# Three pairs of buffers for the attention's result, three for the transposed probabilities, and an order computed anew

## The chip, the cores and the metric

The kernel runs on one core of a Trainium2 chip. The metric is the device time of one execution in microseconds (us); the median of the runs of a kernel is its time, lower is better. The core has TensorE (PE) for matrix products and transposes, VectorE (DVE), ScalarE (ACT) and GpSimd (POOL) for everything elementwise, and SyncE (SP), whose queue issues all transfers here. Each engine takes its instructions strictly in the order in which they were written.

## What is computed

A windowed attention feeds two feed-forward blocks. `x` of 2304 tokens by 512 passes from one to the next.

```python
def _attn_ref(q, k, v):                 # 4 x 8 heads x 576 x 64, a window of 64 positions
    scores = scale * np.matmul(q, k.transpose(0, 1, 3, 2))
    scores = np.where(mask, scores, -1000000000.0)
    attn = np.exp(scores - np.max(scores, axis=-1, keepdims=True))
    attn = attn / (np.sum(attn, axis=-1, keepdims=True) + 1e-09)
    return np.matmul(attn, v).astype(np.float32)

def _moe_ref(x, w_in, w_out, g_ln):     # 512 -> 1024 -> 512
    h = x @ w_in
    solu = h * softmax(h)
    ln = (solu - mu) / np.sqrt(var + 1e-06) * g_ln
    return (ln @ w_out).astype(np.float32)

def _moe2_ref(x, w_in, w_out, a, b):    # 512 -> 2048 -> 512
    P = a[0] + a[1] * h + a[2] * h2 + a[3] * h3
    Q = 1.0 + np.abs(b[0]) * np.abs(h) + np.abs(b[1]) * h2
    return ((P / (Q + 1e-06)) @ w_out).astype(np.float32)
```

The weights arrive as 64-bit floats and are turned into 32-bit ones on the chip.

## The kernel before

The tokens are cut into 18 tiles t of 128. One tile runs through these steps, whose names are the tiles that they write, with the tile's number behind them: the loads `q`, `k` (one each) and `v` (two, v0_0 and v0_1 for tile 0); the scores `s` on PE (L412 adds the mask, L418 the products); the maximum `mx` on DVE (L424), scaled on POOL (L428); eight exponentials `P` on ACT (L433); the sum on POOL (L438), its reciprocal `rc` on DVE (L442), and two halves of a normalization on POOL (L446); two transposes `pt` on PE (L452), copied to `PT` by ACT or DVE (L316, L318); the product with the values `pv` on PE (L472), whose first half needs v0_0 and whose second half needs v0_1; its copy to `xh` and, from tile 2 on, the rest `xl` = pv - xh on DVE (L312). `h` (L577 for tiles 0 and 1, L583 to L585 after) is the first feed-forward product, `st` and `e` (L591 to L633) its activation and layer norm, `pl` (L643) its transposes, `lh` and `ll` their copies. Every third tile closes with four products `x2` (L661 to L663), stored to DRAM. Then the second feed-forward block runs over six blocks of 384 tokens, with the products `hp` (L869 to L871) and `o` (L933 to L935) and an elementwise chain between them.

Beside this, ACT and DVE convert the weights: `xi` to `wi` (L524 to L551), `xo` to `co` and `wo` (L554, L562), and `xc` to `cc`, which go back to DRAM. Each such unit is two passes on ACT and four on DVE, of 1024 columns, and one or two more of each for the split in a high and a low part.

No engine's order is written by hand. `Schedule` (L25) gets every step with its engine, an assumed duration, what it needs, and the rings of buffers that it takes and gives; it works out due times, shifts them by a table of numbers (`SHIFT`, L169), and lets the steps run in a model of the engines. Steps are then written in the order of their modelled start. `RINGS` (L271) holds how many buffers each kind has: "x" is the pair `xh`, `xl` (taken by the step that writes pv, given back by the tile's last `h` product), "PT" the copied probabilities (two per tile, given back by pv), "k" and "q" have two each, given back by the scores, and "s", the scores, has one. A step that takes a buffer that is still held waits on the chip too, and so does everything behind it on its engine. The buffers for `xh` and `xl` stand in a pool of their own (`ax`, L328).

## Time and profile before

| what | before |
|---|---|
| median of 3 runs | 716.35 us (716.21 to 716.68) |
| the profiled execution | 717.4 us |
| its span, first to last instruction | 715.3 us |
| PE busy | 691.1 us (97%) |
| DVE busy | 575.5 us (80%) |
| ACT busy | 488.1 us (68%) |
| POOL busy | 89.0 us (12%) |

The busy times are shares of the span. PE is nearly always busy, so the questions are where the remaining microseconds of PE stand, and which engine ended each of those waits. A busy share over the whole span says little on that, since the stages differ: the first 80 us load, convert weights and run attention, the last 400 us are two products and their elementwise chain.

### The profile page before, as it was taken

The page shows a single profiled execution, that of the slowest core. Times are in us where ns is not written, and L with a number is a line of the kernel's source. Part 1 is how long each engine was busy: PE and PEld are TensorE (multiplying, and loading weights), DVE is VectorE, ACT ScalarE, POOL GpSimd, SP SyncE. Part 2 cuts the span into 40 slices and gives each one's busy share as a digit, 9 for nine tenths or more (in the row PEclk, how much of TensorE's full clock was granted, in tenths as well). Part 3 has the DMA queues.
Part 4 walks back from the last instruction along what each step waited for, and adds up shares of the span by engine and source line. Part 5 has one row for each costly group of instructions (what it writes and reads, how often), then busy time and mean ns, then how long its engine had stood idle before and what let it go on. Part 6 is the DMA issues. An engine that isn't in the chain of part 4 may idle for free.

```text
span 715.3 us, 11585 instructions
## 1 busy us (share of the span) xinstructions
PE 691.1 (97%) x4520; PEld 612.9 (86%) x4520; DVE 575.5 (80%) x713; ACT 488.1 (68%) x918; POOL 89.0 (12%) x142
## 2 busy tenths in 40 slices
PE   2889999999999999999999999999999999999998
PEld 1557899888898899998889988998898889989986
DVE  6899977898999735759998988798598869866973
ACT  6999967768868554748786665766486558555662
POOL 2553332243223220000000000000000000000000
PEclk9999999999999999999999999999999999999999
DMA  9864559668764314426301000200020000001001
GB/s 327 283 218 162 178 202 306 217 215 308 270 231 168 116 45 145 150 68 197 100 22 59 20 1 22 67 1 11 12 68 1 22 30 16 0 1 46 1 0 44
DMA packets 42741, 77.81 MB, mean 109 GB/s; under 512 B 4480, under 2 KB 22912, under 8 KB 42304
## 3 DMA queue, kind: packets, MB, share of 16 engines
q1 hardware_dynamic: 42688, 77.09, 32.1%
q8 instruction: 35, 0.57, 0.3%
q14 instruction: 18, 0.15, 0.1%
HBM read 59.25 MB, written 17.83 MB: 108 GB/s over the span
## 4 chain that ended last, share of the span: by engine, by line
PE 87%; DVE 5%; ACT 4%; DMA 2%; issue 1%; POOL 1%; DVEq 0%; ACTq 0%; POOLq 0%
PE hp L871 8%; PE hp L869 8%; PE hp L870 8%; PE o L935 8%; PE o L934 8%; PE o L933 8%; PE x L661 5%; PE x L663 5%; PE x L662 5%; PE h L583 4%; PE h L584 4%; PE h L585 4%; PE pv L472 3%; PE pl L643 2%; PE pt L452 2%; PE s L418 2%
## 5 line engine op out<-in xcount | busy, mean ns | idle before, releaser
L869 PE MATMUL hp<-x2h,w 128*128 128x384 f32 x384 | 129.4, 337 | 0.7 <-DVE t L902 0.5
L871 PE MATMUL hp<-x2h,w 128*128 128x384 f32 x384 | 129.3, 337 | 0.0
L870 PE MATMUL hp<-x2l,w 128*128 128x384 f32 x384 | 129.2, 337 | 0.0
L935 PE MATMUL o<-w,gl 128*128 128x512 f32 x282 | 111.5, 395 | 0.1
L934 PE MATMUL o<-w,gh 128*128 128x512 f32 x282 | 111.0, 394 | 0.0
L933 PE MATMUL o<-w,gh 128*128 128x512 f32 x282 | 110.7, 393 | 0.0
L879 ACT ACTIVATE w<-hp,ab 128x768 f32<-128x768 f32 x48 | 43.2, 900 | 70.5 <-PE hp L871 70.5
L887 DVE SCALAR_TENSOR_TENSOR w<-r,b,w 128x768 f32<-128x768 f32 x48 | 48.8, 1017 | 37.0 <-ACT r L881 36.9
L869 PEld LDWEIGHTS hp<-x2h,w 128*128 128x128 f32 x384 | 72.1, 188 | 4.0 <-PE hp L871 0.8
L870 PEld LDWEIGHTS hp<-x2l,w 128*128 128x128 f32 x384 | 72.1, 188 | 2.7
L871 PEld LDWEIGHTS hp<-x2h,w 128*128 128x128 f32 x384 | 72.1, 188 | 0.0
L917 ACT CAST gh<-t 128x768 fp32r<-128x768 f32 x48 | 40.1, 835 | 46.8 <-PE o L934 23.8
L661 PE MATMUL x<-lh,wo 128*128 128x384 f32 x192 | 66.7, 348 | 0.0
L663 PE MATMUL x<-lh,wo 128*128 128x384 f32 x192 | 65.0, 339 | 0.0
L662 PE MATMUL x<-ll,wo 128*128 128x384 f32 x192 | 65.0, 338 | 0.0
L935 PEld LDWEIGHTS o<-w,gl 128*128 128x128 f32 x282 | 52.9, 188 | 12.7 <-DVE gl L312 0.5
L934 PEld LDWEIGHTS o<-w,gh 128*128 128x128 f32 x282 | 52.9, 188 | 10.0
L933 PEld LDWEIGHTS o<-w,gh 128*128 128x128 f32 x282 | 53.0, 188 | 9.6
L312 DVE TENSOR_TENSOR gl<-t,gh 128x768 fp32r<-128x768 f32 x48 | 45.8, 954 | 13.8 <-ACT gh L917 13.8
L433 ACT ACTIVATE P<-s,mx 128x128 f32<-128x128 f32 x144 | 52.0, 382 | 2.4 <-POOL mx L428 2.4
L892 ACT ACTIVATE r<-w,qe 128x768 f32<-128x768 f32 x48 | 45.5, 947 | 9.7 <-DVE w L887 9.6
L583 PE MATMUL h<-wi,xh 128*128 128x512 f32 x128 | 50.8, 397 | 0.1
(112 smaller groups left out, 1465.5 us busy)
## 6 DMA issues: line engine op xcount, KB each, us to landing
v<-in_v_dram SPq DMA_DIRECT2D x35, 256.0 KB, 4.1
xc<-in_moe_w_in_dram SPq DMA_DIRECT2D x16, 512.0 KB, 4.4
xc<-in_moe_w_out_dram SPq DMA_DIRECT2D x16, 512.0 KB, 5.4
w2d<-cc SPq DMA_DIRECT2D x16, 512.0 KB, 3.5
r<-w2d SPq DMA_DIRECT2D x16, 512.0 KB, 4.0
k<-in_k_dram SPq DMA_DIRECT2D x17, 384.0 KB, 5.5
q<-in_q_dram SPq DMA_DIRECT2D x18, 256.0 KB, 5.6
x2d<-xs SPq DMA_DIRECT2D x6, 768.0 KB, 4.4
```

Source lines behind the costliest of these rows:

```text
L433: nc.scalar.activation(Pn[t][:, j, n, :], tiles["s", t][:, j, n, :], AF.Exp, bias=mx[:, c:c + 1], scale=0.125, accum_out=su[:, c:c + 1])
L583: nc.tensor.matmul(o, xh[:, c, :], wh, start=(c == 0), stop=False)
L661: nc.tensor.matmul(o, wh, lh[:, f, :], start=(f == 0), stop=False)
L662: nc.tensor.matmul(o, wh, ll[:, f, :], start=False, stop=False)
L663: nc.tensor.matmul(o, wl, lh[:, f, :], start=False, stop=(f == FC1 - 1))
L869: nc.tensor.matmul(h, wh[:, sl], xh[:, c], start=(c == 0), stop=False)
L870: nc.tensor.matmul(h, wh[:, sl], xl[:, c], start=False, stop=False)
L871: nc.tensor.matmul(h, wl[:, sl], xh[:, c], start=False, stop=(c == KC - 1))
L887: nc.vector.scalar_tensor_tensor(out=w, in0=r, scalar=b1, in1=w, op0=ALU.mult, op1=ALU.add)
L933: nc.tensor.matmul(o, gh[:, n, sl], wh, start=(f == 0), stop=False)
L934: nc.tensor.matmul(o, gh[:, n, sl], wl, start=False, stop=False)
L935: nc.tensor.matmul(o, gl[:, n, sl], wh, start=False, stop=(f == FC2 - 1))
```

## The change

The ring "x" grows from two to three pairs and its pool moves to another side of the on-chip memory, where it is closed together with the first feed-forward block. The ring "PT" shrinks from four to three. Some of the durations that the planner assumes are changed, and the table of shifts is another one, so that the order of every engine is another. What is computed, and how many instructions of each kind compute it, stays, apart from some copies that move between ACT and DVE.

```diff
 SHIFT = {
-    "zeros.0": 1.38, "load_q.0": 6.55, "load_k.0": -28.63, "load_v0.0": 141.12, "load_v1.0": -6.38,
...
+    "zeros.0": -13.05, "load_q.0": -5.7, "load_k.0": -7.11, "load_v0.0": 180.85, "load_v1.0": 15.6, "scores.0": 6.51,
...
-RINGS = {"q": 2, "k": 2, "v": 4, "s": 1, "P": 2, "tr": 2, "PT": 4, "o": 2, "x": 2, "h": 1, "e": 2, "lnT": 2, "xs": 1,
+RINGS = {"q": 2, "k": 2, "v": 4, "s": 1, "P": 2, "tr": 2, "PT": 3, "o": 2, "x": 3, "h": 1, "e": 2, "lnT": 2, "xs": 1,
...
-    ax = ctx.enter_context(tc.tile_pool(name="ax", bufs=2))
     ap = att.enter_context(tc.tile_pool(name="ap", bufs=2))
     mp = moe1.enter_context(tc.tile_pool(name="mp", bufs=2, side="right"))
+    ax = moe1.enter_context(tc.tile_pool(name="ax", bufs=3, side="right"))
...
-        PTs[t, j] = ap.tile([P, NPAIR, P], F32, name=f"PT{t}_{j}", tag="PT", bufs=4)
+        PTs[t, j] = ap.tile([P, NPAIR, P], F32, name=f"PT{t}_{j}", tag="PT", bufs=3)
...
-        step("max_scale", "POOL|DVE", (0.33, 0.18), ["max"], max_scale, t)
+        step("max_scale", "POOL|DVE", (0.5, 0.18), ["max"], max_scale, t)
...
-            step(f"norm{j}", "POOL", 1.12, ["rcp"], soft_norm, t, j)
+            step(f"norm{j}", "POOL", 1.3, ["rcp"], soft_norm, t, j)
...
-        step("solu_exp", "ACT", 1.25, ["solu_max"], solu_exp, t)
+        step("solu_exp", "ACT", 1.34, ["solu_max"], solu_exp, t)
...
-        act, ts, tt = (0.61, 0.42, 0.68) if half else (1.06, 0.8, 1.22)
+        act, ts, tt = (0.61, 0.42, 0.68) if half else (1.16, 0.7, 1.22)
```

Three places of the new order, each before and after. Line numbers after are one smaller than before from the changed pool on. The first place is SP's queue, behind the first eight issues (equal in both): the loads of tiles 0 to 4. Before the change it reads:

```order
L383 DMA q2_226<-in_q_dram 128x512
L396 DMA v0_0_106<-in_v_dram 64x512
L390 DMA k3_241<-in_k_dram 128x4x192
L390 DMA k2_253<-in_k_dram 128x4x192
L398 DMA v0_1_257<-in_v_dram 128x512
L498 DMA xo_1_262<-in_moe_w_out_dram 128x512 x2
L398 DMA v1_0_295<-in_v_dram 128x512
L383 DMA q4_326<-in_q_dram 128x512
```

SP's queue at the same place after the change:

```order
L389 DMA k2_225<-in_k_dram 128x4x192
L389 DMA k3_233<-in_k_dram 128x4x192
L395 DMA v0_0_106<-in_v_dram 64x512
L497 DMA xo_1_253<-in_moe_w_out_dram 128x512 x2
L397 DMA v0_1_266<-in_v_dram 128x512
L382 DMA q2_271<-in_q_dram 128x512
L749 DMA gT_98<-in_moe_g_ln_dram 128x8x1
L497 DMA xo_2_279<-in_moe_w_out_dram 128x512 x2
```

The loads v0_0 and q2 moved behind the second of the two `k` loads, and v0_1 moved behind the 1 MB of xo_1.

The second place is ACT, around the copies of tile 4's transposed probabilities (PT4_0, PT4_1). Before the change it reads:

```order
L316 CAST lh0_521<-pl1_1_707 128x4x128
L554 ACTIVATE wo_0_712<-co_0_517,gT_98 128x512
L595 ACTIVATE e2_740,st2_739<-h2_643,st2_739 128x1024
L316 COPY PT4_1_761<-pt4_1_752 128x512
L316 COPY PT4_0_771<-pt4_0_765 128x512
```

ACT at the same place, the copies for pv4, after the change:

```order
L432 ACTIVATE P5_712,sum5_714<-s5_716,mx5_713 128x128 x3
L523 ACTIVATE cc_15_786<-xc_15_709 128x1024
L620 ACTIVATE st2_706<-st2_706 128x1
L621 ACTIVATE st2_706<-st2_706 128x1
L525 ACTIVATE xc_15_709<-xc_15_709 128x1024
L553 ACTIVATE wo_3_816<-co_3_616,gT_98 128x512
L315 COPY PT4_0_830<-pt4_0_809 128x512
L315 COPY PT4_1_857<-pt4_1_822 128x512
```

The two copies moved behind tile 5's eight exponentials and behind a conversion of weights; on PE, h3, s6 and the transposes of tile 4 now stand between s5 and pv4.

The third place is DVE, around xl4, the low part that the product h4 needs. Before the change it reads:

```order
L633 TENSOR_SCALAR e2_740<-e2_740,st2_739 128x1024
L600 ISA e3_844,st3_843<-h3_774,e3_844 128x1024
L600 ISA st3_843 128x1
L602 TENSOR_SCALAR st3_843<-st3_843 128x1
L312 TENSOR_TENSOR xl4_822<-pv4_823,xh4_821 128x512
L424 TENSOR_REDUCE mx6_851<-s6_854 128x8
```

DVE at the same place, up to xl4, after the change:

```order
L632 TENSOR_SCALAR e2_707<-e2_707,st2_706 128x1024
L423 TENSOR_REDUCE mx6_833<-s6_836 128x8
L599 ISA e3_828,st3_827<-h3_760,e3_828 128x1024
L599 ISA st3_827 128x1
L601 TENSOR_SCALAR st3_827<-st3_827 128x1
L311 TENSOR_TENSOR xl4_868<-pv4_869,xh4_867 128x512
```

The maximum of tile 6 moved ahead of xl4. On PE only pl2's eight transposes stand between pv4 and h4 now; before, s6 and pt5 stood there too.

## Rows read from the trace of the kernel before

**Rows 1.** The page, part 1: busy time, share of the span, instructions

```profile
PE 691.1 (97%) x4520; PEld 612.9 (86%) x4520; DVE 575.5 (80%) x713; ACT 488.1 (68%) x918; POOL 89.0 (12%) x142
```

**Rows 2.** Waits of PE, whole span: line, releaser, us in total, times, longest

```profile
PE s L412 <- ACT P L433: 6.2, 1, 6.2
...
PE pv L472 <- ACT PT L316: 3.3, 2, 1.9
PE s L418 <- DMA q<-in_q_dram: 3.2, 1, 3.2
PE pt L452 <- POOL P L446: 2.3, 5, 1.0
...
PE hp L869 <- DVE t L902: 0.5, 1, 0.5
```

**Rows 3.** Busy us by stretch: PE, PEld, DVE, ACT, POOL, clock, DMA share, GB/s

```profile
47.40:60.30 12.90, 11.50 (x145) 9.60 (x144) 12.46 (x20) 12.72 (x34) 4.10 (x7) 1.00 0.69 218
120.00:250.00 130.00, 130.00 (x1204) 115.32 (x1203) 113.88 (x160) 96.76 (x258) 38.34 (x62) 1.00 0.65 226
```

**Rows 4.** Timeline of SP, 11 to 21 us: start, us, issue

```profile
11.14 7.95 SPq L390 DMA_DIRECT2D k<-in_k_dram  x2
19.13 0.51 SPq L398 DMA_DIRECT2D v<-in_v_dram  x1
20.63 0.43 SPq L398 DMA_DIRECT2D v<-in_v_dram  x1
```

**Rows 5.** Landing of the two v issues at 19.13 and at 20.63, in order

```profile
DMA to landing us min/median/max: 3.9/3.9/3.9
...
DMA to landing us min/median/max: 6.0/6.0/6.0
```

**Rows 6.** Timeline, 19 to 48 us: start, us, engine, line, operation, idle before

```profile
19.02 2.11 PE L452 MATMUL pt<-ident,P 128*128 128x128 f32 x8 [0.37 <-POOL P L446]
...
23.44 1.97 PE L472 MATMUL pv<-PT,v 128*64 128x64 f32 x30 [1.90 <-ACT PT L316]
25.77 1.92 PE L418 MATMUL s<-k,q 64*64 64x128 f32 x32
27.62 7.96 PE L577 MATMUL h<-xi,xh 128*128 128x512 f32 x16
...
37.11 2.83 POOL L446 TENSOR_TENSOR P<-P,rc 128x512 f32<-128x512 f32 x2 [1.61 <-DVE rc L442]
...
40.49 7.08 PE L577 MATMUL h<-xi,xh 128*128 128x512 f32 x16
```

**Rows 7.** Timeline, 50 to 54 us: tile 3's copies on ACT, then pv3

```profile
50.48 0.61 ACT L316 CAST xh<-pv 128x512 fp32r<-128x512 f32 x1
...
51.99 1.12 ACT L316 COPY PT<-pt 128x512 f32<-128x512 f32 x2
...
53.16 1.15 PE L472 MATMUL pv<-PT,v 128*64 128x64 f32 x32 [1.40 <-ACT PT L316]
```

**Rows 8.** Timeline, 61 to 77 us: s5, h3, conversions on ACT, pv4, pl2, xl4

```profile
61.09 1.04 PE L418 MATMUL s<-k,q 64*64 64x128 f32 x32
...
64.89 0.50 PE L583 MATMUL h<-wi,xh 128*128 128x512 f32 x1
...
69.17 1.19 ACT L524 ACTIVATE cc<-xc 128x1024 f32<-128x1024 f32 x1
...
70.56 1.15 PE L472 MATMUL pv<-PT,v 128*64 128x64 f32 x32
...
70.68 1.32 ACT L554 ACTIVATE wo<-co,gT 128x512 fp32r<-128x512 f32 x2
...
74.62 1.15 PE L643 MATMUL pl<-ident,e 128*128 128x128 f32 x8 [0.68 <-ACT PT L316]
...
75.23 0.68 DVE L312 TENSOR_TENSOR xl<-pv,xh 128x512 fp32r<-128x512 f32 x1
75.83 1.21 DVE L424 TENSOR_REDUCE mx<-s 128x8 f32<-128x1024 f32 x1
```

More of the change, by code (lines that the diff above doesn't have):

```diff
@@ L698, in attention_moe_moe2 @@
         step("max", "DVE", 1.24, ["scores"], soft_max, t)
-        step("max_scale", "POOL|DVE", (0.33, 0.18), ["max"], max_scale, t)
+        step("max_scale", "POOL|DVE", (0.5, 0.18), ["max"], max_scale, t)
         for j in range(2):
             for n in range(4):
-                step(f"exp{j}{n}", "ACT", 0.36, ["max_scale"], soft_exp, t, j, n, give=[("s", t)])
-        step("sum", "POOL|DVE", (0.4, 0.17), [f"exp{j}{n}" for j in range(2) for n in range(4)], soft_sum, t)
-        step("rcp", "DVE", 0.18, ["sum"], soft_rcp, t)
+                step(f"exp{j}{n}", "ACT", 0.37, ["max_scale"], soft_exp, t, j, n, give=[("s", t)])
+        step("sum", "POOL|DVE", (0.5, 0.17), [f"exp{j}{n}" for j in range(2) for n in range(4)], soft_sum, t)
+        step("rcp", "DVE", 0.2, ["sum"], soft_rcp, t)
         for j in range(2):
-            step(f"norm{j}", "POOL", 1.12, ["rcp"], soft_norm, t, j)
+            step(f"norm{j}", "POOL", 1.3, ["rcp"], soft_norm, t, j)
         for j in range(2):
@@ L719, in attention_moe_moe2 @@
             needs += [("cv7", *key, 0) if t >= FIRST else ("cv6", *key) for key in IN_UNITS if key[1] == c]
-            step(f"h{c}", "PE", 1.39 if t >= FIRST else 1.83, needs, h_mm, t, c,
+            step(f"h{c}", "PE", 1.39 if t >= FIRST else 1.75, needs, h_mm, t, c,
                  want=WANT["h"] + 1.385 * c, take=[] if c else [("h", t)], give=[("x", t)] if c == KC - 1 else [])
         step("solu_max", "DVE", 1.22, ["h3"], solu_max, t, take=[("e", t)])
-        step("solu_exp", "ACT", 1.25, ["solu_max"], solu_exp, t)
+        step("solu_exp", "ACT", 1.34, ["solu_max"], solu_exp, t)
         step("solu_mul", "DVE", 1.46, ["solu_exp"], solu_mul, t, give=[("h", t)])
-        step("ln_square", "ACT", 1.25, ["solu_mul"], ln_square, t)
+        step("ln_square", "ACT", 1.4, ["solu_mul"], ln_square, t)
         step("ln_eps", "POOL", 0.6, ["solu_exp"], ln_eps, t)
         step("ln_var", "POOL|DVE", (0.6, 0.2), ["ln_eps", "ln_square"], ln_var, t)
-        step("ln_root", "ACT", 0.4, ["ln_eps", "ln_square"], ln_root, t)
-        step("ln_newton", "DVE", 0.42, ["ln_root", "ln_var"], ln_newton, t)
-        step("ln_apply", "DVE", 0.81, ["ln_newton"], ln_apply, t)
+        step("ln_root", "ACT", 0.52, ["ln_eps", "ln_square"], ln_root, t)
+        step("ln_newton", "DVE", 0.49, ["ln_root", "ln_var"], ln_newton, t)
+        step("ln_apply", "DVE", 0.84, ["ln_newton"], ln_apply, t)
         for hf in range(2):
@@ L767, in convert @@
         for n in range(2 if key[0] == "o" else 1):
-            act, dve = (0.72, 0.75) if key[0] == "o" else (act, tt)
+            act, dve = (0.72, 0.77) if key[0] == "o" else (act, tt)
             needs = [("cv6", *key)] + ([("gT", 0)] if key[0] == "o" else [])
-            add(("cv6.5", *key, n), "ACT", act, None, needs, cv_hi, key, n, group=group)
+            add(("cv6.5", *key, n), "ACT", act if key[0] == "o" else 0.94 * act, None, needs, cv_hi, key, n, group=group)
             add(("cv7", *key, n), "DVE", dve, want, [("cv6.5", *key, n)], cv_lo, key, n,
```

10 lines of the change are left out of this document (5 added, 5 removed), and 181 rows, old and new, of the table SHIFT.

## The prediction, made before the changed kernel ran

> **What bounds the kernel now.** I read the busy times first, then the waits of PE, then the busy time by stretch, then the timeline of the stretches in which PE waits. PE is busy for 691.1 of 715.3 us [rows 1], so about 24 us of the span are not PE's, and an order can win no more than a part of these. The waits of PE say where they stand [rows 2]: at the very start the first constants, then 3.2 us until the first q, 6.2 us until tile 0's exponentials have freed the one score buffer; then 3.3 us for copies of probabilities on ACT and 2.3 us for the normalization on POOL. The timeline has one more, 0.68 us at 74.62 [rows 8]. The rest is the tail after the last product. From 76 us on PE has no wait worth naming: the stretch from 120 to 250 us is full to the last digit (130.00 of 130.00), while DVE has 16 us and ACT 33 us to spare there [rows 3]. In the stretch from 47.4 to 60.3 us it is the other way round: DVE is busy 12.46 and ACT 12.72 of 12.90 us, and PE waits [rows 3]. So the first 76 us are set by loads, ACT and DVE, with PE's order as the meeting place, and everything behind them is PE's own work, whose count is the same in both kernels. A microsecond that PE loses before 76 us is a microsecond of the end, and the same for one won.
>
> What the rings can do follows from this. A third pair of xh and xl could let pv run further ahead of h, but from 76 us on there is no wait of PE to remove, and none of the waits before it names these buffers as its releaser. The third ring alone is worth 0. The smaller PT ring makes the second copy of tile t+1 wait for pv of tile t; in the new order PE has the transposes of that second half behind pv wherever I looked up to tile 11, so this too is 0 by itself. The time is made by the order of the first 76 us.
>
> **The change, step by step, against the profiled execution (717.4 us; the median of the runs is 716.35, so 1.05 us come off at the end).**
>
> *The start: +3.0 us.* Up to tile 0's transposes ACT, DVE and PE have the same order in both. SP does not. Each k load takes a buffer of an older tile, and the second of the two k loads waits for the scores of tile 1: the two issues stretch from 11.14 to 19.09 us [rows 4]. Before, v0_0 and q2 stand ahead of this wait, and v0_1 is the first behind it, issued at 19.13 and landed 3.9 us later, at 23.0 [rows 4, 5]. Now v0_0 has that place, xo_1 (1 MB) follows, and v0_1 gets the place of the issue at 20.63, which landed after 6.0 us [rows 4, 5]; q2 follows it. So v0_1 lands at about 26.6. The second half of pv0 needs v0_1: it starts at 26.6, not about 24.5, and lasts 16/30 of 1.97 us, to 27.65. s2 takes from the end of pv0 to the start of h0, 25.41 to 27.62 or 2.2 us [rows 6]: it ends at 29.85. Then the new order has the first transposes of tile 1, half of 2.11 us at the slow clock [rows 6], so h0 starts at 30.9 and not 27.62: 3.3 us. Since 128 KB less stand ahead of v0_1 than ahead of the load whose place it takes, I take 3.0. The lower bound: if v0_1 lands after 3.9 us, at 24.5, nothing waits for it, but tile 1's reciprocal stands behind two more DVE passes over 1024 columns (an estimate from the two DVE operations of [rows 8], 0.68 and 1.21 us), so its normalization comes out 1.2 us later, one of the passes having stood in an idle place and the transposes with it; h0 then starts about 1.7 us later. The upper bound adds to 3.3 what the slow clock may cost (below), +3.8. That tile 1's first transposes are already done gives nothing back: after h0 the path runs through DVE's maximum, tile 2's reciprocal, 2.83 us of POOL and the transposes to h1, 4.9 us from 35.6 to 40.49 [rows 6], in the same order in both.
>
> On the clock: s2's 32 products take 1.92 us at 25.77 and s5's 1.04 us at 61.09 [rows 6, 8], so PE is at the lower of its two levels, 1.2 GHz, until inside h0, though the clock column reads 1.00. The new wait lies in this slow stretch, and I count no extra loss for it (at most 0.9 us, what h0 takes above h1: 7.96 against 7.08 [rows 6], half of which I put into the upper bound).
>
> *pv3: -0.5 us.* PE waits 1.40 us for tile 3's copies, which stand on ACT behind the copy of xh2, 0.61 us [rows 7]. The new order gives xh2 to DVE. I take a little less than the copy, since it overlaps its neighbours; bounds 0 and -0.7.
>
> *s5 to h3: -1.9 us.* Before, tile 4's transposes stand between s5 (ends 62.13) and h3 (64.89): 2.76 us for eight transposes, which take about 0.9 us when nothing holds them (pl2's eight, 1.15 from the first start to the last end) [rows 8]; the rest is waiting for POOL. Now h3 follows s5, and its 5.7 us (64.89 to 70.56) cover the normalization. If POOL is late, -1.0.
>
> *pl2: -0.7 us*, the wait at 74.62 [rows 8], since other waits stand ahead of it now.
>
> *pv4: +1.9 us.* The copies of tile 4's probabilities moved on ACT behind tile 5's exponentials and a conversion. From the end of s5 to the end of tile 5's exponentials took 7.0 us before (62.13 to 69.17, with two copies of 1.1 us in it) [rows 7, 8]; without them 5.9. Then follow two conversion passes at 1.1 (1.19, overlapping a little), two small operations and half of a wo pair (1.32) at 1.1 together, and the copies at 1.1 us: 10.3 us after s5. PE's work in that time is h3 5.7, eight transposes 0.9, s6 1.3 and half of pt5's eight 0.45: 8.35. PE is 1.95 us early; I take 1.9. What hides this cost if ACT is ahead is h3; bounds 0.5 and 3.
>
> *h4: +1.2 us.* Before, xl4 started at 75.23, about when h4 wanted it [rows 8]. Now h4 stands 0.9 us behind pv4, and between them come a copy (xh4, 0.6) and xl4 (0.68), and on DVE the maximum of tile 6 (1.21) and the product for e3 (1.2) stand ahead of xl4. At the least 0.4 us, at the most 2.2.
>
> The sum is 3.0 - 0.5 - 1.9 - 0.7 + 1.9 + 1.2 = +3.0 us. Behind h4 I count 0: there the products x2 begin, which ask little of DVE and ACT. At the change to the second block PE waits 0.5 us now [rows 2], and 3 us more for ACT and DVE can only shorten that. 717.4 + 3.0 - 1.05 = **719.4 us**.
>
> **The Trainium skill on the loads.** The places in rows 4 and 5 land in the order of issue. "DMA: Bandwidth & Descriptors", section "Queues, rings and completion order", says that completion is not first-in first-out per issuing engine. By that rule v0_1 could overtake xo_1 and land after 3.9 us; the start would then cost 1.7 and not 3.0 us, and the sum would be 1.7 instead of 3.0.
>
> **The rivals.**
> *Early loads, same time.* v0_1 and q2 land some 4 us after their issue, the start costs 1.7, pv4 and h4 come at 1.0 and 0.5: 1.7 - 3.1 + 1.5 = +0.1, 716.4. For it: the issue at 19.13 landed that fast behind a k load [rows 4, 5]. Against it: xo_1's megabyte is issued right before v0_1.
> *Faster, ACT and DVE in time.* The waits at pv4 and h4 do not come (they decide from 2 us of work that ACT and DVE have done earlier, because PE's late start gave them time), the start is 1.7 to 2: 2.0 - 3.1 - 0.5 for the wait at the second block = -1.6, 714.8. For it: ACT and DVE are what bound here, and PE's delay gives them time. Against it: DVE itself waits for s2 and h0, and gets two more copies of 0.68 us.
> *Worse.* Every upper bound of start, pv4 and h4 holds, or a wait appears between 85 and 360 us, where in the new order the second transposes of several tiles stand only one group of transposes and one of scores ahead of their pv: 3.8 + 3 + 2.2 - 3.1 = +5.9 at the most, of which I take 5.0, 721.4.
> *The change does nothing that counts*: the rings are 0 in all cases, as worked out above, and only the order makes the time; the forecast is already that case.
>
> **How the numbers follow.** The forecast (718 to 721.3) 0.58, early loads 0.22, faster 0.12, worse 0.08. Within 0.2% of the median, 714.9 to 717.8, is about what a measurement of this kernel cannot tell from no change. The forecast's range lies above 717.8; the faster rival lies half outside 714.9 but its variants with a smaller start also belong to it. So faster 0.12, same 0.22, slower 0.66. For 8 times in 10 the range takes in early loads and leaves out the faster rival and the far end of the worse one: 715.5 to 722.0. The likeliest case alone spans 718.0 to 721.3.
>
> **What the profile after would show.** Right: v0_1 lands at 26 us or later, PE waits for a load at pv0, h0 starts at 30 to 31 us; the waits of pt4 on POOL are gone; new waits stand at pv4 (ACT copies) and at h4 (xl4 on DVE), together some 3 us; from 85 us on PE is full. Wrong: h0 starts before 29.5 us, or pv4 and h4 follow without a wait; or PE waits behind 85 us, which no term here holds.

## The result, and the profile after

The changed kernel takes 726.89 us (median of three runs, 726.54 to 726.93) against 716.35: the ratio is 1.0145, with a 95% interval of 1.0122 to 1.0168. The forecast was 719.4 with a range of 715.5 to 722.0, so the direction was right and the size was not: 10.5 us instead of 3.0. Five more runs of the changed kernel, made later beside 22 of the kernel before, gave 724.80 (724.13 to 727.19) against 717.13 (715.98 to 718.86), ratio 1.0111 (1.0094 to 1.0129), or 7.7 us. Of the 2.8 us between these two distances 0.8 lie in the kernel before (716.35 and 717.13); the rest lies in how single executions of the changed kernel went, of which the clock of TensorE can explain a part (below). So each kernel below is compared with the kernel before on the same chip, in the same batch of runs, and kernels of different batches by their distances from it (the changed kernel: 7.7 us).

The profiled execution of the changed kernel took 726.93 us, its span is 725.0. The page's first part, busy time, share of the span and instructions of each engine; before, it is [rows 1]:

```profile
PE 695.0 (96%) x4520; PEld 615.1 (85%) x4520; DVE 579.0 (80%) x715; ACT 489.3 (67%) x917; POOL 89.5 (12%) x141
```

What PE waited for (line that waits, releaser: us in total, times, longest); before, it is [rows 2]:

```profile
PE s L417 <- DVE xi L535: 3.3, 1, 3.3
PE h L582 <- DVE st L599: 3.2, 1, 3.2
PE o L932 <- ACT os L315: 3.1, 4, 0.8
PE pv L471 <- DMA v<-in_v_dram: 3.0, 1, 3.0
PE pv L471 <- ACT PT L315: 2.7, 2, 2.0
PE pt L451 <- POOL P L445: 0.9, 3, 0.4
```

Three of them are new: one load, one wait of h for DVE, and four waits of o for a copy on ACT, in the second block, where the forecast had a zero. (The 3.3 us put down to DVE stand where 3.2 us were put down to the first q.) PE is also busy 3.9 us longer (695.0 for 691.1) for the same products. The span has grown by 9.7 us (725.0 for 715.3): slower products are 3.9 of it, and idle time of PE the other 5.8.

The start, from the timeline of PE (start, us, engine, line, operation, idle before and its releaser); before, h0 started at 27.62 and h1 at 40.49 [rows 6]:

```profile
23.09 1.12 PE L471 MATMUL pv<-PT,v 128*64 128x64 f32 x16 [1.98 <-ACT PT L315]
27.17 1.12 PE L471 MATMUL pv<-PT,v 128*64 128x64 f32 x16 [2.95 <-DMA v<-in_v_dram]
...
28.65 1.92 PE L417 MATMUL s<-k,q 64*64 64x128 f32 x32
30.50 1.12 PE L451 MATMUL pt<-ident,P 128*128 128x128 f32 x4
31.41 7.84 PE L576 MATMUL h<-xi,xh 128*128 128x512 f32 x16
...
43.68 7.08 PE L576 MATMUL h<-xi,xh 128*128 128x512 f32 x16
```

This part came as forecast: v0_1 was issued at 20.80, landed 6.3 us later at 27.1 (26.6 in the forecast), h0 started at 31.4 (30.9), and h1 is 3.2 us late (3.0 to 3.3).

Then tile 3's h, on the same timeline (the products of s ahead of it are s5):

```profile
63.67 1.04 PE L417 MATMUL s<-k,q 64*64 64x128 f32 x32
67.91 0.76 PE L582 MATMUL h<-wi,xh 128*128 128x512 f32 x1 [3.19 <-DVE st L599]
68.47 0.63 PE L583 MATMUL h<-wi,xh 128*128 128x512 f32 x1
...
74.01 0.40 PE L584 MATMUL h<-wi,xl 128*128 128x512 f32 x1
...
76.34 1.04 PE L451 MATMUL pt<-ident,P 128*128 128x128 f32 x8
```

The same place in the busy time by stretch (us, PE busy and its instructions, granted clock, DMA share, GB/s):

```profile
66.00:68.00 2.00, 0.10 (x1) 0.79 1.03 386
68.00:72.00 4.00, 4.00 (x10) 0.50 0.56 181
72.00:74.00 2.00, 2.00 (x6) 0.50 0.04 8
74.00:76.00 2.00, 2.00 (x10) 1.00 0.15 27
```

PE waits 3.19 us, the granted clock falls to 0.50 (1.2 GHz) in that wait and is back at 1.00 (2.4 GHz) only at 74 us, though PE is busy all the time from 68 us on. The 24 products of h3 take from 67.91 to 76.34, 8.43 us, where before they took 5.67 (64.89 to 70.56, [rows 8]): 2.76 us that no term of the forecast held.

What h3 waits for is seen on the timeline of DVE and ACT in the same stretch, after (the step of the last row also writes st, the name in the list of waits):

```profile
62.77 1.22 DVE L590 TENSOR_REDUCE st<-h 128x1 f32<-128x1024 f32 x1
...
64.69 1.11 ACT L594 ACTIVATE e<-h,st 128x1024 f32<-128x1024 f32 x1
64.80 1.23 DVE L423 TENSOR_REDUCE mx<-s 128x8 f32<-128x1024 f32 x1 [0.21 <-PE s L417]
...
66.53 1.22 DVE L599 CUSTOM_DVE_ANT_0 e<-h,e 128x1024 f32<-128x1024 f32 x1
```

The last of these on the timeline of DVE before, with the row that ends it:

```profile
63.61 1.21 DVE L600 CUSTOM_DVE_ANT_0 e<-h,e 128x1024 f32<-128x1024 f32 x1
64.75 0.08 DVE L600 DVE_READ_ACCUMULATOR2_ANT st<- 128x1 f32 x1
```

There is one buffer for h. Tile 2's h stands in it until DVE has multiplied it with its exponential (the row e<-h,e), and only then can h3 begin: at 67.91 behind 67.75 after, at 64.89 behind 64.83 before. In both kernels the chain is maximum of h (st), exponential (e<-h,st), product. Before, tile 4's transposes and their waits for POOL filled the time, and the profile named POOL as the releaser.

In the second block of the layer, at the change from one block of rows to the next (timeline of ACT and PE; it is the same at 536.94, 604.66 and 672.65):

```profile
463.59 1.07 ACT L315 COPY os<-o 128x512 f32<-128x512 f32 x2
...
466.81 0.90 ACT L878 ACTIVATE w<-hp,ab 128x768 f32<-128x768 f32 x1 [2.15 <-PE hp L870]
...
467.61 0.80 ACT L880 ACTIVATE r<-hp 128x768 f32<-128x768 f32 x1
...
468.30 0.59 ACT L315 COPY os<-o 128x512 f32<-128x512 f32 x1
...
468.94 0.50 PE L932 MATMUL o<-w,gh 128*128 128x512 f32 x1 [0.78 <-ACT os L315]
```

The three results of a block stand in three buffers, which the next block's first o needs. Two copies are done at once; the third stands on ACT behind two activations of the next hp, and while these wait, ACT is idle for 2.15 us. PE has 24 products of hp between the last o of a block and the first of the next (462.45 to 466.62, 4.2 us). Before, PE had 48 there (452.01 to 460.33, 8.3 us), and the third copy stood behind one activation; it was done at 457.74, 2.6 us ahead of the first o:

```profile
456.36 0.91 ACT L879 ACTIVATE w<-hp,ab 128x768 f32<-128x768 f32 x1 [1.10 <-PE hp L871]
457.16 0.58 ACT L316 COPY os<-o 128x512 f32<-128x512 f32 x1
```

Without the wait this third o would have started at 468.00: 0.94 us, and 0.11 more until the products run at their pace, make 1.05 us, four times.

### The profile page after: what moved, and what is told of

It is laid out like the page before. It is cut to its first block, busy times and chain, and to the rows that moved or that the text cites. A ratio compares the mean times of both kernels' runs of the same rounds, so it can differ in the third digit from the quotient of the medians.

```text
span 725.0 us, 11579 instructions
## 1 busy us (share of the span) xinstructions
PE 695.0 (96%) x4520; PEld 615.1 (85%) x4520; DVE 579.0 (80%) x715; ACT 489.3 (67%) x917; POOL 89.5 (12%) x141
## 3 DMA queue, kind: packets, MB, share of 16 engines
q1 hardware_dynamic: 42688, 77.09, 31.4%
## 4 chain that ended last, share of the span: by engine, by line
PE 94%; ACT 2%; DMA 1%; DVE 1%; issue 1%; POOL 0%; SPq 0%; POOLq 0%
PE hp L870 9%; PE hp L869 9%; PE hp L868 9%; PE o L932 9%; PE o L934 9%; PE o L933 9%; PE x L660 5%; PE x L662 5%; PE x L661 5%; PE h L582 4%; PE h L584 4%; PE h L583 4%; PE pv L471 3%; PE pl L642 2%; PE s L417 2%; PE pt L451 2%
## 5 line engine op out<-in xcount | busy, mean ns | idle before, releaser
L582 PE MATMUL h<-wi,xh 128*128 128x512 f32 x128 | 52.6, 411 | 3.2 <-DVE st L599 3.2
L583 PE MATMUL h<-wi,xh 128*128 128x512 f32 x128 | 51.8, 405 | 0.0
L584 PE MATMUL h<-wi,xl 128*128 128x512 f32 x128 | 51.7, 404 | 0.0
```

What stands on the lines that cost most here:

```text
L582: nc.tensor.matmul(o, xh[:, c, :], wh, start=(c == 0), stop=False)
L583: nc.tensor.matmul(o, xh[:, c, :], wl, start=False, stop=False)
L584: nc.tensor.matmul(o, xl[:, c, :], wh, start=False, stop=(c == KC - 1))
```

## Experiments

Lines are counted anew in each kernel, so L582 of the changed kernel is L594 where twelve lines stand ahead of it. Steps are moved in the order that the planner has made: a pair (step, other) puts the step right ahead of the other one, whatever engine it runs on. My theory was now that the loss is made of separate places (start, wait at h3, clock behind it, block changes); its main rival, that ACT and DVE bind, and that what one place gives is lost at the next.

### The clock behind the wait at h3, and whether it always falls

```diff
+    def warm(n):
+        o = po.tile([P, NPAIR, P], F32, name="warm", tag="o")
+        for i in range(n):
+            nc.tensor.matmul(o, ib, masks[:, 0, :].unsqueeze(1).broadcast_to([P, NPAIR, P]), start=True, stop=True)
...
+WARM = {('h0', 3): 14}
```

The table gives the step ahead of which such products stand, and their number; they multiply constants, and nothing reads them.

> The changed kernel with 14 products of constants put on PE between tile 5's scores and tile 3's h; they go to a PSUM buffer that nothing reads. In the changed kernel PE stands idle there from 64.7 to 67.9 us and tile 3's h then takes 8.43 us instead of 5.67, with a granted clock of 0.50. Theory 'the wait drops the clock': with PE busy (14 products at about 0.21 us, 3.0 us in all) h starts at the same 67.9 us, takes 5.7 us, and the time falls by 2.5 to 2.8 us, to about 724.2. Rival 'the slow stretch has another cause' (the loads that run at 1.03 to 1.06 of the queues' share from 66 to 70 us, or the products of this tile themselves): h takes 8.4 us again and the time stays at 726.9, or grows if the added products push h.

724.96 us (724.62 to 726.91) against 717.26, ratio 1.0116 (1.0100 to 1.0131). In its profile the clock stays at 1.00 and h3 takes its 5.7 us; but then PE waits 0.36 us ahead of tile 5's transposes and 0.75 us ahead of h4. The span is 2.3 us under that of the changed kernel's first profile: 0.9 of it is an earlier start (h1 at 42.82 for 43.68), and 1.5 is the stretch from the start of h3 to the start of h4, 11.78 us for 13.27. That is below the 2.5 to 2.8 expected, since the slow h3 had hidden these two waits. The rival with the loads falls: they ran as before. But the median is 7.7 us over the kernel before, as the changed kernel's own is in its later runs: by the median, keeping the clock up here gained nothing.

The changed kernel itself was then run again.

> The changed kernel itself once more. Of the runs of one and the same kernel on the start, three had a span of 721.5 us and three one of 724.6 to 725.0: theory 'whether the clock falls in the wait at tile 3's h differs from execution to execution'. It expects for the changed kernel spans near 725 where it falls and near 722 where it does not, that is times of 726.5 to 727 and of 723 to 724, and a median between 723 and 727 with this chance. Rival 'this kernel always loses the clock there, since its wait lies at a fixed time': all runs 726.5 to 727, and then the kernel with the old rings, at 722.4 to 724.3, is faster because of its rings.

724.80 us against 717.13: spans of 722.3, 722.5, 722.9, 724.3 and 724.8. Its profile has the same wait of 3.19 us, and here the clock does not fall:

```profile
68.50 0.47 PE L582 MATMUL h<-wi,xh 128*128 128x512 f32 x1 [3.19 <-DVE st L599]
...
76.79 0.63 PE L451 MATMUL pt<-ident,P 128*128 128x128 f32 x4 [0.35 <-ACT PT L315]
...
80.28 0.47 PE L582 MATMUL h<-wi,xh 128*128 128x512 f32 x1 [0.76 <-ACT lh L315]
```

The granted clock in the same place, and the row on DVE that ends the product with tile 3's h:

```profile
68.00:70.00 2.00, 1.50 (x7) 1.00 1.04 343
70.00:74.00 4.00, 4.00 (x19) 1.00 0.19 67
```

```profile
80.06 0.08 DVE L599 DVE_READ_ACCUMULATOR2_ANT st<- 128x1 f32 x1
```

So one and the same wait takes the clock in one execution and not in the next. Of six profiles with this wait of 3.19 us two have the fall (the first one of the changed kernel, and the run on the loads) and four do not. In the two profiles of the changed kernel the stretch from h3 to h4 takes 13.27 and 11.78 us, so the fall is worth 1.5 us of the end (2.76 less the two waits that it hides). It does not explain the scatter alone: the profile without the fall has one of the two long spans (724.3), since its start was late (h1 at 44.27, against 42.82 in the run before it), and one of the four runs with products in the wait has a span of 725.0. What the executions without a profile did is not shown.

The 0.76 us at h4 are put down to ACT's copy of lh, which h4 does not read. The one buffer of h fits better: in all twelve profiles of the changed order, with and without moved steps, h4 starts 0.15 us behind the end of DVE's product with tile 3's h (80.14 and 80.28 here), and the copy of lh ends anywhere from 0.08 to 17 us ahead of it. In the kernel before, this distance is 0.40 us, and h4 does not wait. So h4 stands at the same buffer as h3.

### The wait at h3

```diff
+MOVES = [
+    (('solu_exp', 2), ('cv6.5', 'o', 0, 0)),
+    (('solu_mul', 2), ('max', 5)),
+]
```

> The changed kernel with two steps of tile 2 moved ahead: its exponential on ACT ahead of a conversion pass (0.73 us), its product on DVE ahead of tile 5's maximum (1.23 us, which itself waits for tile 5's scores) and of half of ll. Theory 'h waits for the one h buffer, which tile 2's product frees': the product ends about 1.1 us earlier, h starts at about 66.8 us instead of 67.9, the wait shrinks from 3.2 to 2.1 us; the time falls by 1.1 us if the clock falls all the same (725.8) and by up to 3.9 us if it does not (723.0). Rival 'h waits for xl3 or for the loads': h starts at 67.9 us as before and the time is 726.9. Second rival: the gain is lost again at pv4, whose copies wait on ACT behind tile 5's later exponentials: 726 to 727 with a new wait at pv4.

725.65 us, 1.0120 (1.0105 to 1.0135). In its profile PE waits 1.98 us at h3 instead of 3.19, again named as the product on DVE: h waits for that buffer, and the rivals xl3 and loads fall. But the time is lost at the next places: tile 4's transposes wait 1.13 us for POOL, those of tile 5 1.35 us for a copy, h4 0.76. The second rival of that expectation has it, though it put the new wait at pv4. The clock stayed up in this profile, and still the median is 8.4 us over the kernel before: nothing was won. A single place in this stretch can't be valued by itself.

### The start

```diff
+MOVES = [
+    (('load_q', 2), ('load_k', 2)),
+    (('load_v0', 0), ('load_k', 2)),
+    (('load_v1', 0), ('cvl', 'o', 1)),
+]
```

> The changed kernel with three loads issued where the kernel before has them: q2 and the first half of v0 ahead of the k loads of tiles 2 and 3, the second half of v0 ahead of the megabyte of the weights. Theory 'the start costs 3 us of the end': PE's wait at pv0 (2.95 us) goes, tile 0's h starts at 28.2 to 28.6 us instead of 31.4, and all that follows comes about 3 us earlier: 723.9, with the wait at tile 3's h and the slow clock unchanged. Rival 'the early stretch is bound by ACT and DVE, so what PE gains is waited off': the start comes 3 us earlier but the waits at pv3 and h3 grow by the same amount: 726 to 727.

724.49 us, 1.0107 (1.0093 to 1.0121), which is 7.2 us over the kernel before for the changed kernel's 7.7. The load's wait is gone, and PE now waits for POOL at tile 1's first transposes, which the new order has ahead of h0:

```profile
28.69 1.12 PE L462 MATMUL pt<-ident,P 128*128 128x128 f32 x4 [1.16 <-POOL P L456]
29.60 8.55 PE L587 MATMUL h<-xi,xh 128*128 128x512 f32 x16
```

h0 comes 1.8 us earlier than in the changed kernel, not 3; it is 2.0 us later than before, near the lower bound of the forecast's first step (1.7). With h0 slower (8.55 us) h1 comes only 1.1 us earlier. With these transposes and their copy behind h0 as well:

```diff
 MOVES = [
...
+    (('probs0', 1), ('probs1', 1)),
+    (('probs_copy0', 1), ('cv6.5', 'o', 1, 1)),
 ]
```

> The changed kernel with the start as before in both of its parts: the three loads at their old places (as in the run on the loads) and tile 1's first transposes behind tile 0's h instead of ahead of it, where PE waited 1.16 us for POOL once the load's wait was gone. Theory 'the start costs 3 us of the end, and is made of the loads and of these transposes': h of tile 0 starts at 27.6 us as before, that of tile 1 at 40.5 to 41 instead of 43.7, the time is 723.5 to 724 with the slow clock at tile 3's h and 721 to 721.5 without it. Rival 'the chain over DVE's maximum and POOL sets tile 1's h': it starts at 42 us or later and the time is 724.5 as with the loads alone.

724.97 us (723.37 to 726.84), 1.0106 (1.0086 to 1.0127), in two groups: three runs at 723.4 and three at 726.5 to 726.8, spans of 721.5 and of 724.6 to 725.0. The second group has no profile, and its distance of 3.1 us is more than a fall of the clock at h3 makes; what sets it apart is not shown. The profile is of the first group, with the clock up at h3. In it h0 starts at 28.78 and h1 at 40.74, a quarter of a microsecond behind the kernel before. What keeps h0 from 27.6 is the copy of xh0 on ACT, behind two conversion passes (wait 1.62 us). h3 starts at 65.83 with its 3.19 us of waiting, h4 at 77.61: 0.94 and 2.08 us later than before [rows 8]. From h4 on it loses another 4.1 us, the size of the four block changes (4 x 1.05; the other terms behind h4 nearly cancel, as the account below shows). That is the whole of its span over the kernel before, 721.5 - 715.3 = 6.2 us.

### The block changes

```diff
+MOVES = [
+    (('oc', 1, 2), ('g_pre0', 19)),
+    (('oc', 2, 2), ('g_pre0', 27)),
+    (('oc', 3, 2), ('g_pre0', 35)),
+    (('oc', 4, 2), ('g_pre0', 43)),
+]
```

> The changed kernel with the third copy of a block's result moved on ACT ahead of the next pair's first activation, at the four block changes where PE waits 0.78 us for it. Theory 'PE waits four times for this copy, and each wait is the end's': the four waits go, 726.9 - 3.1 = 723.8. Rival 'the copy only waits for the store of the first result at its new place, and now the activation behind it is late': the waits stay or move to the products that follow, 726 to 727.5.

720.35 us (719.92 to 722.62) against 717.26, 1.0051 (1.0037 to 1.0065): 3.1 us over the kernel before instead of 7.7, or 4.6 won. All four waits of o are gone; ACT now waits for the store of the block's first result instead, in time it had idle anyway (the third copy, on the timeline of ACT):

```profile
463.75 0.59 ACT L327 COPY os<-o 128x512 f32<-128x512 f32 x1 [1.69 <-DMA out_dram<-os]
```

This was the largest single place, and PE's releaser names it outright.

### The rings alone, and the place in memory

```diff
-    ax = ctx.enter_context(tc.tile_pool(name="ax", bufs=2))
...
     mp = moe1.enter_context(tc.tile_pool(name="mp", bufs=2, side="right"))
+    ax = moe1.enter_context(tc.tile_pool(name="ax", bufs=3, side="right"))
...
-        PTs[t, j] = ap.tile([P, NPAIR, P], F32, name=f"PT{t}_{j}", tag="PT", bufs=4)
+        PTs[t, j] = ap.tile([P, NPAIR, P], F32, name=f"PT{t}_{j}", tag="PT", bufs=3)
```

> The kernel before with its own order, and only the rings of the changed one: three pairs of xh and xl (in the place in memory that the changed kernel gives them), three PT. Theory 'the rings alone are worth 0': the same time as before within what the runs scatter, no new wait of PE. Rival 'the smaller PT ring costs': the second copy of a tile waits for the pv of the tile before, PE waits for PT between 23 and 80 us, 0.5 to 2 us slower. Rival 'the third pair gains': pv starts earlier somewhere, 0.5 us or more faster.

718.65 us against 717.78, ratio 1.0015 (1.0007 to 1.0024): not zero. PE's waits are those of the kernel before (the one at hp is shorter, 0.2 us for 0.5). But the places drift apart: pv of tile 2 is 0.28 us early, pv of tile 17, at 269 us, 1.71 us late. Nearly all of it lies in the products h<-wi. The other way round, the new order with the old rings (the same diff turned about):

> The changed kernel with its own order, and only the rings of the kernel before: two pairs of xh and xl, four PT. Theory 'the rings alone are worth 0, the order makes the time': 726.5 to 727 (or 724 to 725 where the clock does not fall behind tile 3's h). Rival 'the new order needs the third pair': pv waits for xh or xl of two tiles before, and the time grows by 0.5 us or more.

723.14 us (722.36 to 724.33) against 717.78, 1.0084 (1.0069 to 1.0099): 5.4 us over the kernel before instead of 7.7, faster than the 724 to 727 expected, and no wait for xh or xl: no place of the new order needs the third pair. To tell the place from the number, three more kernels: two pairs on the other side, behind the pool of e and lh (the diff above with bufs=2 and PT as before); three PT and nothing else; two pairs on the other side ahead of that pool.

> The kernel before with its own order and its own counts (two pairs of xh and xl, four PT); only the memory of xh and xl is taken where the changed kernel takes it, on the other side, behind the pool of tile 0's and later e and lh. In all profiles with the new rings each of the 384 products h<-wi with xh or xl comes 234 ns behind the one before it, in all with the old rings 227 ns. Theory 'the place does it': 234 ns, and about 2 us over the kernel before. Rival 'the third pair or the shorter PT ring does it': 227 ns and the time of the kernel before.

> The kernel before with three PT instead of four and nothing else. Theory 'the place of xh and xl makes h's products slower': they stay at 227 ns and the time is that of the kernel before. Rival 'the PT ring does it' (its memory lies behind that of xh and xl): 234 ns and about 2 us more.

> The kernel before with the memory of its two pairs of xh and xl on the other side, as in the run on the place, but ahead of the pool of e and lh instead of behind it. If the place decides, it shows whether the side does (234 ns again) or the address on that side (227 ns).

Against 716.95 of the kernel before: 718.69 us (1.0027, 1.0016 to 1.0037), 717.42 (1.0005, 0.9996 to 1.0013) and 718.59 (1.0024, 1.0015 to 1.0033). The groups of instructions by line (busy time, mean ns of one), one line each of the kernel before, of three PT alone and of two pairs in the new place:

```profile
L584 PE MATMUL h<-wi,xh 128*128 128x512 f32 x128 | 50.0, 391 | 0.0
```

```profile
L584 PE MATMUL h<-wi,xh 128*128 128x512 f32 x128 | 50.0, 391 | 0.0
```

```profile
L584 PE MATMUL h<-wi,xh 128*128 128x512 f32 x128 | 50.7, 396 | 0.0
```

From the starts, each such product follows the one before after 227 ns with the old place and after 234 ns with the new one, in each of the 16 tiles and in every profile. 384 x 6.6 ns = 2.5 us, of which 0.9 (the rings alone), 1.7 and 1.6 (the two places) show in the time. In their profiles the last x2 is 1.6 to 1.9 us late, and 0.7 to 1.0 of it comes back at the change to the second block, where the kernel before has a wait that is shorter here. The place does it, not the third pair and not PT. The pools opened behind it move too, but of the other products none is slower (h1 takes 7.08 us at either place). What about the new address is slower, these runs do not tell (the second place on that side is as slow).

### Do the places add up?

Start and block changes mended by the two lists above, and 14 products of constants at h3:

> The changed kernel with three of the places mended at once: the start (loads and tile 1's transposes as before), the third result copy at the block changes, and 14 products of constants in the wait at tile 3's h so that the clock stays. Theory 'the places add up': 723.4 (the start mended, clock up) less 4 x 1.05 for the block changes gives 719.2, and it does not scatter by 3 us, since PE does not stand idle at h3. Rival 'what one place gives is lost at the next': over 721.

721.88 us (720.54 to 722.93), 1.0061 (1.0047 to 1.0076): 2.9 us under the changed kernel, 2.7 over what was expected, and in the range of the rival (over 721). The profile shows where it went: h0 took 10.00 us instead of 7.1, since the granted clock was 0.50 from 28 to 32 us, and one block change kept a wait of 0.58 us. The start, mended, has again a wait (1.12 us for xh0) and a clock that falls or rises late.

Start and block changes mended, and tile 4's transposes ahead of h3 as before:

```diff
 MOVES = [
...
+    (('rcp', 4), ('ln_lo0', 1)),
+    (('ln_lo1', 1), ('max', 5)),
+    (('norm0', 4), ('max_scale', 5)),
+    (('norm1', 4), ('max_scale', 5)),
+    (('probs0', 4), ('exp01', 5)),
+    (('probs1', 4), ('exp01', 5)),
+    (('probs_copy0', 4), ('exp01', 5)),
+    (('probs_copy1', 4), ('exp01', 5)),
 ]
```

> The changed kernel with the start and the block changes mended, and tile 4's transposes, their copies and the steps that they need (reciprocal, normalization, the second half of ll) ahead of tile 3's h, as in the kernel before. Theory 'what is left of the change is the order around tile 3's h: h waits for its one buffer in both kernels, and before, the transposes filled that wait': PE's wait at h goes from 3.2 us to under 1.5 us in all, the waits at pt and h behind it (0.35 and 0.76) go, and the time is that of the kernel before within 1 us, 716 to 717.5. Rival 'the changed order loses elsewhere too, in waits too short to be listed': over 718.

719.37 us (717.71 to 721.88), 1.0032 (1.0018 to 1.0045). The wait at h3 is now the same group of short ones as before, 1.6 us in all (under 1.5 expected):

```profile
65.02 0.66 PE L476 MATMUL pt<-ident,P 128*128 128x128 f32 x4 [0.69 <-POOL P L470]
66.02 0.66 PE L476 MATMUL pt<-ident,P 128*128 128x128 f32 x4 [0.34 <-POOL P L470]
67.25 0.51 PE L607 MATMUL h<-wi,xh 128*128 128x512 f32 x1 [0.58 <-DVE st L624]
```

From h1 to h3 it takes 24.8 us (42.44 to 67.25), before 24.4. But it is 2.2 us over the kernel before, not within 1 as expected (the rival had over 718): 2 us are the place of xh and xl, and h1 is still 1.95 us late, by the wait for xh0 (1.87) and a slow h0 (8.83); the second block, without the four waits, gives some 2.4 us back. The last two kernels take these away too. The first has all the lists above, the old rings, and products of constants at the start:

```diff
+WARM = {('scores', 0): 6, ('scores', 1): 22, ('attend', 0): 4}
```

> The changed kernel's order with all the places mended (start, tile 3's h, block changes), the old rings, and products of constants in the waits at the start (6, 22 and 4). From the kernel with all places mended (fast executions 716 to 717.5 by span, products h at 234 ns) 2.3 us come off for the 384 products at 227 ns, and 1 to 2 us for the start at the higher clock: 713 to 715. Rival 'the start's gain is lost at the wait for xh0 on ACT', which stood at 1.9 us there: 715 to 717.

The second also has the copy of xh0 moved ahead:

```diff
 MOVES = [
...
+    (('attend', 0), ('cvr', 'i', 3, 0)),
+    (('att_hi', 0), ('cvr', 'i', 3, 0)),
+    (('max', 2), ('cv6', 'i', 3, 0)),
 ]
```

> The run before it (changed order, places mended, old rings, products of constants at the start) had 2.17 us of PE's waiting for the copy of xh0 on ACT, behind two conversion passes, and h of tile 0 at 28.63 us against 27.62 in the kernel before. Here that copy stands ahead of the passes, and tile 2's maximum on DVE ahead of a conversion step of 2.06 us. Theory 'the copy is what is left of the lost start': h starts at 26.5 to 27 us, tile 1's h 1.0 to 1.5 us earlier than in that run (40.7), and the time falls by as much, to about 715.5 (714.5 in the best executions). Rival 'POOL and DVE set tile 1's h': it stays at 40.5 us and the time at 717.

The first: 717.18 us against 716.95, 0.9999 (0.9990 to 1.0009), at the upper end of its rival (715 to 717), with 2.17 us of waiting for xh0. The second: 715.73 against 717.14, 0.9978 (0.9969 to 0.9987). These two have products of constants at the start, which the kernel before lacks; with such products it took 715.37 us beside the second (next section). So with every named place mended the new order stands 0.4 us over the old one with the same help, and nothing large is left unnamed. The step from one to the other is 1.45 us by the median. In the profile h0 came to 26.60 us as expected, but h1 moved by only 0.15 (40.55 for 40.70), as the rival "POOL and DVE set tile 1's h" had it: the time came out as the theory said and the mechanism did not, and most of the step lies in executions without a profile.

### The clock at the start of the kernel before

```diff
+WARM = {('scores', 0): 6, ('scores', 1): 22, ('attend', 0): 8}
```

> The kernel before with products of constants in the waits of PE at the start, into a buffer that nothing reads: 6 ahead of tile 0's scores, 22 behind them, 8 ahead of pv0. Before, PE's products are at the lower clock until inside tile 0's h. Theory 'the clock is low there because PE has stood idle': the scores of tile 1 take 1.0 instead of 1.9 us, the transposes of tile 0 1.1 instead of 2.1, pv0 1.15 instead of 1.97, h of tile 0 7.1 instead of 7.96; what ACT and POOL leave of that at the end is 1 to 2.7 us, 713.7 to 715.3 against 716.3. Rival 'the clock rises at a time of its own, whatever PE does': the 22 products take 0.43 us each and push tile 1's scores by 3 us; the time is the same or up to 3 us longer.

715.05 us (715.00 to 715.32) against 717.78, ratio 0.9968 (0.9956 to 0.9980): faster than both kernels. From its timeline and its busy time by stretch:

```profile
8.21 1.10 PE L423 MATMUL s<-k,q 64*64 64x128 f32 x32 [0.60 <-DVE xi L548]
...
16.26 0.41 PE L417 MATMUL s<-masks,ib 64*64 64x512 bf16 x4 [2.09 <-ACT P L438]
...
18.98 2.12 PE L457 MATMUL pt<-ident,P 128*128 128x128 f32 x8 [1.44 <-POOL P L451]
...
26.05 1.04 PE L423 MATMUL s<-k,q 64*64 64x128 f32 x32
```

```profile
18.00:20.00 2.00, 1.02 (x5) 0.57 1.05 255
20.00:22.00 2.00, 2.00 (x8) 0.50 1.06 393
```

The scores take 1.04 to 1.10 us instead of 1.9, h0 starts at 27.02 and takes 7.13 (7.96 before, [rows 6]), h1 starts 0.97 us earlier, h4 0.92. But the span is 2.2 us shorter (713.1 for 715.3). The other 1.3 us come between 345 and 364 us, at the change to the second block. There ACT waits for a load of weights, and behind ACT and DVE PE loses these 1.3 us in the kernel before (the 0.5 us at hp in [rows 2] are a part of them) and next to none here. The copy on ACT that waits, before and here:

```profile
355.46 1.05 ACT L824 CAST w<-r 128x1024 fp32r<-128x1024 f32 x1 [3.50 <-DMA r<-w2d]
```

```profile
352.98 1.05 ACT L836 CAST w<-r 128x1024 fp32r<-128x1024 f32 x1 [2.16 <-DMA r<-w2d]
```

The load landed 4.9 us after its issue before and 3.6 us here; in the three profiles of the old order with products at the start it took 3.4 to 3.7 us, in the five without 4.2 to 4.9. Whether the products have a part in that is not shown. Nor is the start itself all gain: behind two waits of 2.09 and 1.44 us the clock falls at 19 us, and the transposes of tile 0 are slow again. To close these waits:

```diff
-WARM = {('scores', 0): 6, ('scores', 1): 22, ('attend', 0): 8}
+WARM = {('scores', 0): 6, ('scores', 1): 30, ('probs0', 0): 5, ('attend', 0): 11}
```

> The kernel before with more products of constants at the start: 6 ahead of tile 0's scores, 30 behind them, 5 ahead of tile 0's transposes, 11 ahead of pv0, so that PE has next to no idle time between 4.3 and 24 us. In the run with 6, 22 and 8 the clock fell to 0.50 at 19 us, behind idle times of 2.1 and 1.4 us, and tile 0's transposes took 2.12 us, pv0 started 1 us late at 24.43. Theory 'the clock falls because PE stands idle': the clock stays at 1.00, the transposes take 1.1 us, pv0 starts at 23 to 23.5 us, h of tile 0 at 25.6 to 26, and the time is 0.5 to 1.5 us below that run, 713.6 to 714.6. Rival 'it falls at a time of its own': the transposes take 2.1 us again, the products ahead of pv0 push it to 25 us, and the time is 715 to 716.

715.18 us (715.01 to 717.29), 0.9975 (0.9966 to 0.9984): the transposes now take 1.04 us, but in its profile the clock had not yet risen for tile 0's scores (1.99 us), and the 30 products behind them, 8.07 us long, pushed tile 1's scores to 18.1. Closing the waits brings nothing more: the rival's time (715 to 716), though not its reason, since the transposes are fast. The first of the two, repeated:

> The kernel before with 6, 22 and 8 products of constants in the waits at the start, once more beside the run above. Theory 'the clock at the start is worth about 2 us to the kernel before': 714.9 to 715.4 again, with less scatter than the kernel before, whose runs went from 715.7 to 718.5. Rival 'that was a lucky set of executions': a median over 716.

715.37 us (714.99 to 716.92) against 717.14, 0.9981 (0.9972 to 0.9989). The gain repeats, with 1.8 us after 2.7; in its profile, too, 1.0 us is at h1 and 1.3 at the change to the second block.

Here the Trainium skill, "TensorE: Matmul & The Clock Gate", section "What's actually happening", fits it: there the low level is the default, and PE's recent activity releases it, by a clockwork that does not start with the kernel. The trace agrees with the first (with products in the waits the scores run at full pace) and with the second as far as it shows it (one wait of 3.19 us with a fall, and the same wait without; and tile 0's scores, behind the same six products in the first two of these kernels, take 1.10 us in one and 1.99 in the other).

## Why the prediction was wrong, by its own steps

*The start, +3.0: right in the trace.* 3.2 us at h1. Taken out, it won less: 0.5 us by the median (7.2 over the kernel before for 7.7), in runs that spread over 3.5 us. The Trainium skill, "DMA: Bandwidth & Descriptors", section "Queues, rings and completion order", says that completion is not first-in first-out per issuing engine; the prediction took from it that the load might overtake the megabyte. The trace doesn't show that: xo_1's two halves landed ahead of it (issued from 19.70 on, 5.2 to 6.1 us), and it came at 27.1. What I had not seen is the copy of xh0 behind more conversion passes on ACT: behind the load's wait a second and a third one stood, and each showed only when the one ahead of it had gone.

*pv3, -0.5: right* (the wait is 0.73 us instead of 1.40).

*s5 to h3, -1.9: wrong, and the step that failed first.* It said "h3 follows s5 now, and its 5.7 us cover the normalization". h3 can't follow: its one buffer is held by tile 2 until DVE's product, whose end before, 64.83, stands 0.06 us ahead of h3's start. I took the releaser that the profile named for the waits in that stretch, POOL, for the bound, and did not ask what the moved instruction itself needs. From pv3 to h3 the lag grew by 0.5 us (2.52 to 3.02) where it should have shrunk by 1.9. The transposes put back ahead of h3 left 0.58 us of the 3.19 at h3.

*The clock, +0: wrong.* I counted only the start. The unfilled wait at h3 took the clock in the profiled execution: 2.76 us at h3, 1.5 of it left at h4. In the later profile it did not.

*pl2, pv4 and h4, -0.7 + 1.9 + 1.2 = +2.4: mis-sized.* With the slow h3 none of the waits was left (5.78 us late at h3's end, 5.65 at h4). At the full clock they are 0.35 and 0.76, at pt5 and h4, for 1.9 and 1.2, and from h3 to h4 the lag grows by 1.1 us. At h4 it is not xl4 that holds, as the prediction had it, but the buffer of h once more. ACT and DVE gained time while PE waited for the buffer, which is what the rival "ACT and DVE in time" said.

*The rings, 0: wrong in size, and for a reason outside the argument.* No wait changed, as said; the new place of xh and xl makes 384 products 6.6 ns longer, 2.5 us of products, of which 0.9 to 1.7 us showed in the time.

*Behind h4, 0: wrong.* "Ask little of DVE and ACT" holds on the average of the stretch, and not at the block changes: 4 x 1.05 = 4.2 us. The other products of the second block gave back some 2.4: the distances from start to start add up to 1.25 us less for hp and 1.2 less for o beside the four waits. Some 1.4 of that is what the kernel before itself loses between 345 and 364 us.

From h4's start on: 4.2 + 2.2 (14 tiles at the new place) + 0.5 (transposes of tile 5 still to do) - 2.4 = 4.5, against 9.7 - 5.65 = 4.05 read; some 0.4 us stays open. The prediction had named two of these signs as showing it wrong, "pv4 and h4 follow without a wait" and "PE waits behind 85 us", and both came in the first profile. No rival held the measured time: "worse" with all its upper bounds ends at 717.4 + 5.9 - 1.05 = 722.3 us, since none had a term for the buffer of h, for a clock that falls at h3, or for the block changes behind 460 us.

## What to carry to other kernels

Where an order is changed, take each product that moves up and list what it needs itself, the buffer that it writes into first: a wait that the profile puts down to something else may be standing on top of it. The same distance to one event in every profile (0.15 us at h4) says more than the name of the releaser. Look at each change of block by itself, because a stretch that is full on the average tells nothing of the one copy that stands behind the next block's activations. And price an idle time of PE of 2 to 3 us at its length and at a possible clock loss behind it; products of constants made the kernel before 1.8 to 2.7 us faster, of which its profiles show 1.0 at the start where they stand; in the wait at h3 they kept the clock up and gained nothing by the median.

## What the hardware showed that I had not expected

- The place of the stationary operand in memory changes the pace of fp32r products of 128x512: 227 ns from start to start at the old place of xh and xl, 234 at two places on the other side, with the same data and the same loads of weights (188 ns at either place).
- The same wait of 3.19 us brought the granted clock to 0.50 in two profiles and left it at 1.00 in four; in the first it stayed down for 6 us of full work (68 to 74 us). In the kernel with every place mended it fell where the three waits ahead of h3 were only 0.82, 0.34 and 0.58 us long: 0.50 from 66 to 68 us.
